# Order of ScalarE's copies, routing counts and a second expert's steps in an attention kernel with two expert layers

## The chip, the cores and the metric

The kernel runs on one core of one Trainium2 chip (trn2). The metric is the device time of one execution in microseconds, of which three were taken: median 483.18 us, lowest 483.08, highest 484.01.

## The reference

Three layers in sequence, all in fp32. (1) Attention over q, k, v of shape 2 x 8 x 768 x 64 with a local window of 96 keys, 8 global keys and a linear bias per head:

```python
scores = scale * np.matmul(q, k.transpose(0, 1, 3, 2))
scores = np.where(keep, scores + bias[None, :, :, :], -1000000000.0)
a = np.exp(scores - np.max(scores, axis=-1, keepdims=True))
out = np.matmul(a / (np.sum(a, axis=-1, keepdims=True) + 1e-09), v)
```

(2) A routed layer: each of the 1536 rows (512 wide) goes to one of 8 experts. A gate decides per row whether it takes its own best expert or that of the row before it. The result is `p[e] * (np.maximum(x @ w1[e], 0) @ w2[e])`, with 512 x 1024 and 1024 x 512 weights per expert. (3) A mixing layer: rows are mixed with the row before them, then `r * (k * k @ w_v)` with `k = np.maximum(xk @ w_k, 0)` and `r` a sigmoid of `xr @ w_r`.

## The kernel before, in words

The program is written under a manual schedule: each engine runs its instructions in the order in which the code emits them, and waits in that order. `n` holds the tensors and routing helpers (class `Net`); the body of `build` emits everything.

**Attention.** 12 tiles t of 128 query rows, each in two halves g of 4 heads: 24 steps i = 2t + g, of which 23 run in the loop `for i in range(NI - 1)` and the last behind it. In a step there are these pieces:

- `emit_S(u)` (L900): scores of step u, 8 products from `strip` (the turned keys, in the trace under zbig) and `qz` (turned, scaled queries). Even u write two S banks, odd u the banks T and O.
- `emit_min(u)` (L914, VectorE): adds the bias table, takes the row minimum of the negated scores, writes the tiles pe (peb, peexh, peexl, or parts of zbig).
- `emit_exp(u, b)` (L926, ScalarE): exponentials with row sums.
- `emit_pT(u, b)` (L933, L935, TensorE): turns the probabilities into a PT bank; `emit_ev(u, b)` copies that bank to pt, for b = 0 on VectorE (L944), for b = 1 on ScalarE (L942).
- `emit_pv(u, b)` (L958): products of pt with v; vp is the part of the tile before. `emit_xT(t)` (L963, ScalarE) copies the finished O bank; `n.turn_x` (L185) turns it and `n.route_x` (L189, VectorE) scales it to the rows X.
- `turn4` (L857) turns the next tile's k and q into two S banks, and `emit_kT` (L862) and `emit_qT` (L866) copy them on ScalarE to `strip` and `qz`.

An odd step from 3 on is "late": it emits the scores of both steps of the next tile, then exponentials, the probabilities of the step before, and so on. An even step turns k and q of the next tile first, then the probabilities of the step before; ScalarE does half of the step's exponentials, the copy pt, the other half, and then the two copies of k and q. The products with v of both halves of a tile end the even step, and the next step's scores follow.

**Routing inside attention.** Tiles go in pairs (groups). Each group runs through gate logits (`route_lgt`, L211), maxima (`route_max`, `route_max2`, tile ab), rows (`route_rows`, L263, ScalarE copy br at L266), a scan over the rows (`route_scan`, L274), turning back (`route_turn`, L282), one-hots (`route_oh`), sums (`route_sum`), positions (`pos`, which computes posi and lets the rows be scattered to xs in DRAM) and a running count (`route_acc`). `plan` is a table: `at(i, point, ...)` registers a function at a named point of step i, `do(i, point)` runs it there. The points of a step in order are Ra, E0 (even steps), Dm, Rb, Db, Rc, Dc; minima of the next step stand between Rb and Db in even steps, the products with v between Db and Rc.

After the groups of tiles 4, 5 and of tiles 6, 7 two experts are picked early: `counted` copies counts, `order_a` makes keys (dgf, dgg), `order_k` compares them on TensorE (L347), `order_c` ranks them (`order_b` is both), `early_pick` (L367) and `early_start` give the expert's number to SP's queue, which then loads its weights (wraw). `scatter` of tile 7 is followed by the load xe of gathered rows on SP (L982), which waits for the scattered rows.

**After attention.** The first expert's tile is computed between the last routing steps (`fill`), then all experts, then the mixing layer. `bg_early` loads and splits the first expert's weights in the late steps of attention.

Of the kernel before, what the change touches and what calls it, by code (L numbers as in the profile page):

```python
# [21 lines left out]
NTT = B * NT  # L22
# [27 lines left out]
NI = 2 * NTT  # L50
# [560 lines left out]
def build(ctx, tc, ins, out):  # L611
    n = Net(ctx, tc, ins, out)
# [247 lines left out]
    def emit_kT(t, psv=None):  # L860
        psv = turn4(kn.pop(t)) if psv is None else psv
        nc.scalar.activation(out=strip[:, :, cols(t):cols(t) + P], in_=psv, func=ACTF.Copy)  # L862
# [110 lines left out]
    def early_start(rank, r):  # L973
        fi = n.early_index(rp, rank)
        wsrc[r] = nc.values_load(fi[:, 0:1], engines=(SP,), min_val=0, max_val=E - 1)
# [23 lines left out]
    def at(i, point, *fs):  # L999
        plan.setdefault((i, point), []).extend(fs)  # L1000

    def do(i, point):
        for f in plan.pop((i, point), ()):
            f()

    def pos(g):
        n.route_pos(ap2, g)
        scq.extend(g)
        nm = {3: "cnt4", 5: "cnt6", 7: "cnte", 9: "cnt9", 11: "cnt"}.get(g[-1])
        if nm:  # L1010
            setattr(n, nm, n.counted(rp, g, nm))

    for g in groups:
        i = 2 * g[-1] + 3
        lgg, mx, mx2, rows, scan, tn, oh, sm_, ps_, acc = (lambda f=f, g=g: f(ap2, g) for f in (
            lambda _, g: n.route_lgt(ap2, g, xTs), n.route_max, n.route_max2, n.route_rows, n.route_scan, n.route_turn, n.route_oh, n.route_sum,
            lambda _, g: pos(g), n.route_acc))
        if g[-1] == NTT - 1:
            tail = mx, mx2, rows, scan, tn, oh, sm_, ps_
            continue  # L1020
        at(i, "Rb", lgg)
        at(i + 1, "E0", lambda g=g: n.route_lge(ap2, g))
        at(i + 1, "Rb", lambda g=g: n.route_lgb(ap2, g))
        at(i + 1, "Db", mx, mx2)
        if g[-1] == NTT - 3:
            tail8 = rows, scan, tn, oh, sm_, ps_, acc
            continue
        if g[-1] == NTT - 5:
            at(i + 1, "Rc", rows)
            at(i + 1, "Dc", scan)  # L1030
            at(i + 2, "Ra", tn)
            at(i + 2, "Dm", oh)
            at(i + 2, "Rb", sm_)
            at(i + 2, "Db", ps_, acc)
        else:
            at(i + 2, "Ra", rows)
            at(i + 2, "Dm", scan)
            at(i + 2, "Rb", tn)
            at(i + 2, "Db", oh)
            at(i + 3, "Rb", sm_)  # L1040
            at(i + 3, "Db", ps_, acc)
        if g[-1] in (5, 7):
            e = g[-1] == 7
            at(i + 3 - e, "Db", lambda e=e: n.order_a(ap2, "fg"[e], n.cnte if e else n.cnt6, n.fvec if e else None))
            if e:
                at(i + 3, "Rb", n.order_k)
                at(i + 3, "Db", lambda: n.order_c(ap2, "g", rp))
            else:
                at(i + 3, "Dc", lambda: n.order_b(ap2, "f", rp))
            at(i + 4, "Ra", lambda e=e: n.early_pick(rp, 3 * e))  # L1050
            at(i + 4, "Dm", lambda e=e: early_start(3 * e, e))

    with tc.manual_schedule():
        n.scalars_load(n.const, nc.scalar)
# [98 lines left out]
        for i in range(NI - 1):  # L1153
# [4 lines left out]
            def scores():  # L1158
# [5 lines left out]
                if i == 0:  # L1164
                    emit_kglob(0)

            turned = []
            if late:
                scores()
                emit_xT(t - 1)  # L1170
                emit_exp(i, 0)
                emit_exp(i, 1)
                do(i, "Ra")
                emit_pT(i - 1, 0)
                emit_pT(i - 1, 1)
                n.turn_x(xTs[t - 1], t - 1, "O" if i < NI - 3 else "PT")
                if i < NI - 2:
                    emit_min(i + 1)
                do(i, "Dm")
                emit_ev(i - 1, 0)  # L1180
                emit_ev(i - 1, 1, True)
            else:
                if i and t + 1 < NTT and not g:
                    turned = [turn4(kn.pop(t + 1)), turn4(qn.pop(t + 1))]
                if 0 < i:
                    emit_pT(i - 1, 0)
                    emit_pT(i - 1, 1)
                do(i, "Ra")
                emit_exp(i, 0)
                do(i, "E0")  # L1190
                if 0 < i:
                    emit_ev(i - 1, 0)
                    emit_ev(i - 1, 1, True)
                emit_exp(i, 1)
                if i and g == 0:
                    n.route_ri(t - 1, stat[t - 1][1])
                do(i, "Dm")
# [4 lines left out]
                scores()  # L1202
            if scq:
                scatter(scq.pop(0))
            if g == 0 and t + 1 < NTT:
                emit_kT(t + 1, *turned[0:1])
                if t + 2 < NTT:
                    load("k", t + 2)
                emit_qT(t + 1, *turned[1:2])
                if t + 2 < NTT:  # L1210
                    load("q", t + 2)
            do(i, "Rb")
            bg_early()
            if i < NI - 2 and not late:
                emit_min(i + 1)
# [58 lines left out]
        i = NI - 1  # L1274
# [755 lines left out]
```

## Time and profile before

| what | value |
|---|---|
| median of 3 runs | 483.18 us (483.08 to 484.01) |
| the profiled execution | 482.91 us |
| its span, first to last instruction | 481.0 us |
| TensorE (PE) busy | 457.8 us, 95% |
| weight loads (PEld) busy | 396.4 us, 82% |
| VectorE (DVE) busy | 345.3 us, 72% |
| ScalarE (ACT) busy | 266.8 us, 55% |
| GpSimd (POOL) busy | 116.4 us, 24% |
| granted TensorE clock | 0.999 of full speed |

Attention and its routing take the first 108 us or so of the span, the experts and the mixing layer the rest. Shares over the whole span say little about one part, so the stretches and timelines below are read by part. In a timeline row, the bracket is the time that the engine sat idle before that instruction and what ended it; "issue" there means that the profile shows no releaser.

### The profile page before, as it was taken

The page shows a single profiled execution, that of the slowest core. Times are in us where ns is not written, and L with a number is a line of the kernel's source. Part 1 is how long each engine was busy: PE and PEld are TensorE (multiplying, and loading weights), DVE is VectorE, ACT ScalarE, POOL GpSimd, SP SyncE. Part 2 cuts the span into 40 slices and gives each one's busy share as a digit, 9 for nine tenths or more (in the row PEclk, how much of TensorE's full clock was granted, in tenths as well). Part 3 has the DMA queues.
Part 4 walks back from the last instruction along what each step waited for, and adds up shares of the span by engine and source line. Part 5 has one row for each costly group of instructions (what it writes and reads, how often), then busy time and mean ns, then how long its engine had stood idle before and what let it go on. Part 6 is the DMA issues. An engine that isn't in the chain of part 4 may idle for free. (4 is left out here: it accounts for less than half of the span.)

```text
span 481.0 us, 9252 instructions
## 1 busy us (share of the span) xinstructions
PE 457.8 (95%) x3210; PEld 396.4 (82%) x3210; DVE 345.3 (72%) x911; ACT 266.8 (55%) x657; POOL 116.4 (24%) x204
## 2 busy tenths in 40 slices
PE   7889989899999999999999999999999999999994
PEld 5778778777788989878879887897989898898984
DVE  7777887896967876988898888797757767363301
ACT  4787877893526645667686775852424324152320
POOL 4202112202210000000010013061854819162220
PEclk9999999999999999999999999999999999999999
DMA  8977485785585878598699743003837441200001
GB/s 191 273 210 170 123 212 177 230 271 167 214 281 162 324 247 310 185 341 286 240 343 399 242 166 110 22 1 98 297 110 256 145 172 62 87 2 23 22 3 49
DMA packets 76491, 86.90 MB, mean 181 GB/s; under 512 B 50676, under 2 KB 50932, under 8 KB 76436
## 3 DMA queue, kind: packets, MB, share of 16 engines
q1 hardware_dynamic: 68176, 63.01, 41.6%
q0 software_dynamic: 4944, 17.17, 10.7%
q10 hardware_dynamic: 3316, 6.03, 3.5%
q8 instruction: 28, 0.46, 0.4%
q14 instruction: 27, 0.22, 0.1%
HBM read 73.49 MB, written 12.71 MB: 179 GB/s over the span
## 5 line engine op out<-in xcount | busy, mean ns | idle before, releaser
L659 ACT ACTIVATE whi<-wraw 128x512 fp32r<-128x512 f32 x128 | 72.5, 623 | 6.5 <-ACT yo L778 2.4
L668 DVE TENSOR_TENSOR wlo<-wraw,whi 128x1024 fp32r<-128x1024 f32 x55 | 66.1, 1218 | 2.7 <-ACT whi L659 2.2
L1541 ACT ACTIVATE sq<-S 128x256 f32<-128x256 f32 x48 | 18.4, 384 | 72.8 <-PE S L677 72.6
L675 PE MATMUL S<-xkh,whi 128*128 128x256 f32 x192 | 54.3, 283 | 0.2 <-ACT whi L659 0.2
L677 PE MATMUL S<-xkh,wlo 128*128 128x256 f32 x192 | 53.3, 278 | 0.2 <-DVE wlo L664 0.2
L1551 POOL TENSOR_TENSOR kl<-sq,kh 128x256 fp32r<-128x256 f32 x40 | 36.4, 919 | 69.5 <-issue 36.7
L676 PE MATMUL S<-xkl,whi 128*128 128x256 f32 x192 | 53.2, 277 | 0.0
L1581 DVE TENSOR_TENSOR o<-O,sig 128x512 f32<-128x512 f32 (+1 forms) x13 | 8.4, 650 | 51.0 <-PE O L677 31.7
L676 PE MATMUL O<-wlo,kh 128*128 128x512 f32 (+1 forms) x104 | 39.1, 376 | 0.6 <-DVE wlo L664 0.6
L677 PE MATMUL O<-whi,kl 128*128 128x512 f32 (+1 forms) x104 | 39.2, 377 | 0.0
L675 PE MATMUL O<-whi,kh 128*128 128x512 f32 (+1 forms) x104 | 38.8, 373 | 0.0
L675 PEld LDWEIGHTS S<-xkh,whi 128*128 128x128 f32 x192 | 36.1, 188 | 0.7 <-ACT whi L659 0.4
L677 PEld LDWEIGHTS S<-xkh,wlo 128*128 128x128 f32 x192 | 36.1, 188 | 0.4 <-DVE wlo L664 0.4
L676 PEld LDWEIGHTS S<-xkl,whi 128*128 128x128 f32 x192 | 36.1, 188 | 0.3
L1542 DVE SCALAR_TENSOR_TENSOR sq<-S,sq 128x256 f32<-128x256 f32 x48 | 20.1, 421 | 15.7 <-ACT sq L1541 15.2
L1550 ACT ACTIVATE kh<-sq 128x256 fp32r<-128x256 f32 x48 | 19.7, 412 | 12.8 <-DVE sq L1542 12.8
L676 PEld LDWEIGHTS O<-wlo,kh 128*128 128x128 f32 x104 | 19.6, 188 | 4.9 <-DVE wlo L664 1.1
L675 PEld LDWEIGHTS O<-whi,kh 128*128 128x128 f32 x104 | 19.6, 188 | 3.6
L307 POOL DMA_INDIRECT xs<-X,posi x10 | 11.4, 1141 | 45.9 <-DVE acc L325 22.0
L942 ACT ACTIVATE pt<-PT 128x512 f32<-128x512 f32 (+1 forms) x24 | 13.5, 561 | 16.3 <-PE PT L935 13.7
L677 PEld LDWEIGHTS O<-whi,kl 128*128 128x128 f32 x104 | 19.6, 188 | 3.5
L944 DVE COPY pt<-PT 128x512 f32<-128x512 f32 (+1 forms) x24 | 15.3, 639 | 5.9 <-PE PT L935 4.7
(485 smaller groups left out, 1420.8 us busy)
## 6 DMA issues: line engine op xcount, KB each, us to landing
wraw<-in_moe_w_dram SPq DMA_DIRECT2D x64, 512.0 KB, 5.3
dwt<-in_moe_w_v_dram POOLq DMA_DIRECT2D x8, 512.0 KB, 4.0
z<-in_moe_w_k_dram SPq DMA_DIRECT2D x8, 512.0 KB, 4.4
z<-in_moe_w_v_dram SPq DMA_DIRECT2D x8, 512.0 KB, 4.9
ys<-yo ACTq DMA_DIRECT2D x13, 256.0 KB, 7.0
vn<-in_v_dram SPq DMA_DIRECT2D x12, 256.0 KB, 3.8
xn<-xs SPq DMA_DIRECT2D x12, 256.0 KB, 5.5
dwt<-in_moe_w_k_dram POOLq DMA_DIRECT2D x6, 512.0 KB, 7.4
```

The costliest lines, as they stand in the source:

```text
L307: self.nc.gpsimd.indirect_dma_start(self.xviews[t], bass.IndirectOffsetOnAxis(ap=self.posi[:, t:t + 1], axis=0), X[t], None)
L659: nc.scalar.activation(out=whl[r, c][0][:, sl], in_=raws[r, c][:, sl], func=ACTF.Copy)
L668: nc.vector.tensor_tensor(lo, raws.pop((r, c)), hi.bitcast(F32), op=ALU.subtract)
L675: nc.tensor.matmul(out_, lhsT=ah, rhs=bh, start=first, stop=False)
L676: nc.tensor.matmul(out_, lhsT=ah, rhs=bl, start=False, stop=False)
L677: nc.tensor.matmul(out_, lhsT=al, rhs=bh, start=False, stop=last)
L942: nc.scalar.activation(out=d[:, 0:ps.shape[1]], in_=ps, func=ACTF.Copy)
L944: nc.vector.tensor_copy(d[:, 0:ps.shape[1]], ps)
L1541: nc.scalar.activation(out=sq_, in_=ps[:, 0:TB], func=ACTF.Relu)
L1542: nc.vector.scalar_tensor_tensor(sq_, ps[:, 0:TB], 0.0, sq_, op0=ALU.max, op1=ALU.mult)
L1550: nc.scalar.activation(out=hh, in_=sq_, func=ACTF.Copy)
L1551: (nc.gpsimd if b else nc.vector).tensor_tensor(hl, sq_, hh.bitcast(F32), op=ALU.subtract)
```

## The change

Four edits, all of order:

1. In even steps from 4 on, the copies of the next tile's k and q (with the loads that follow them) move up, in front of the probabilities' copies pt. The step 2, which had k and q turned first, now turns them behind the probabilities, and copies them where it did before.
2. The counts and keys of both early experts (`counted`, `order_a`) are made at Rb of step 16 and of step 20, in front of the minima; `order_k` follows the products with v (Rc), `order_c` at Dc. Before, the first expert's were at Db and Dc of step 16, the second's spread over Db of step 19 and Rb and Db of step 20.
3. The group of tiles 6, 7 loses its own, earlier slots: its rows move from Rc of step 18 to Ra of step 19 (behind the scores), and all later steps of it half a step or a step on, the scatters of tiles 6 and 7 and the load xe from step 19 to step 20.
4. In step 21 the turn of x moves from in front of the minima's place to behind Rb (behind the gate logits).

```diff
     def pos(g):
...
-        nm = {3: "cnt4", 5: "cnt6", 7: "cnte", 9: "cnt9", 11: "cnt"}.get(g[-1])
+        nm = {3: "cnt4", 9: "cnt9", 11: "cnt"}.get(g[-1])
...
-        if g[-1] == NTT - 5:
-            at(i + 1, "Rc", rows)
-            at(i + 1, "Dc", scan)
-            at(i + 2, "Ra", tn)
-            at(i + 2, "Dm", oh)
-            at(i + 2, "Rb", sm_)
-            at(i + 2, "Db", ps_, acc)
-        else:
...
+        at(i + 2, "Ra", rows)
+        at(i + 2, "Dm", scan)
+        at(i + 2, "Rb", tn)
+        at(i + 2, "Db", oh)
+        at(i + 3, "Rb", sm_)
         if g[-1] in (5, 7):
             e = g[-1] == 7
-            at(i + 3 - e, "Db", lambda e=e: n.order_a(ap2, "fg"[e], n.cnte if e else n.cnt6, n.fvec if e else None))
-            if e:
-                at(i + 3, "Rb", n.order_k)
-                at(i + 3, "Db", lambda: n.order_c(ap2, "g", rp))
-            else:
-                at(i + 3, "Dc", lambda: n.order_b(ap2, "f", rp))
+
+            def count(g=g, e=e):
+                nm = "cnte" if e else "cnt6"
+                setattr(n, nm, n.counted(rp, g, nm))
+                n.order_a(ap2, "fg"[e], getattr(n, nm), n.fvec if e else None)
+
+            at(i + 3, "Rb", count)
+            at(i + 3, "Db", ps_, acc)
+            at(i + 3, "Rc", n.order_k)
+            at(i + 3, "Dc", lambda e=e: n.order_c(ap2, "fg"[e], rp))
...
+            def next_kq(*turned):
+                emit_kT(t + 1, *turned[0:1])
+                if t + 2 < NTT:
+                    load("k", t + 2)
+                emit_qT(t + 1, *turned[1:2])
+                if t + 2 < NTT:
+                    load("q", t + 2)
...
-                n.turn_x(xTs[t - 1], t - 1, "O" if i < NI - 3 else "PT")
+                if i < NI - 3:
+                    n.turn_x(xTs[t - 1], t - 1, "O")
...
-                if i and t + 1 < NTT and not g:
+                if i > 2 and t + 1 < NTT and not g:
                     turned = [turn4(kn.pop(t + 1)), turn4(qn.pop(t + 1))]
...
                 emit_exp(i, 0)
                 do(i, "E0")
+                if turned:
+                    next_kq(*turned)
                 if 0 < i:
                     emit_ev(i - 1, 0)
                     emit_ev(i - 1, 1, True)
...
-            if g == 0 and t + 1 < NTT:
-                emit_kT(t + 1, *turned[0:1])
-                if t + 2 < NTT:
-                    load("k", t + 2)
-                emit_qT(t + 1, *turned[1:2])
-                if t + 2 < NTT:
-                    load("q", t + 2)
+            if g == 0 and t + 1 < NTT and not turned:
+                next_kq()
             do(i, "Rb")
+            if late and i == NI - 3:
+                n.turn_x(xTs[t - 1], t - 1)
```

What the change moves, at three places. ScalarE in step 6, before (lgt are the gate logits, zbig and qz the copies of k and q, peexh and peexl the two halves of the exponentials):

```order
L926 ACTIVATE peexh,sm_561<-peexh,nm_560 128x232 x2
L218 ACTIVATE lgt_605<-R_570 128x256
L942 ACTIVATE pt_1_609<-PT_598 128x512
L926 ACTIVATE peexl,sm_561<-peexl,nm_560 128x232 x2
L862 ACTIVATE zbig<-S_583 128x4x128
L866 ACTIVATE qz<-S_588 128x512
L963 ACTIVATE xT_676<-O_644 128x512
```

and with the change:

```order
L926 ACTIVATE peexh,sm_561<-peexh,nm_560 128x232 x2
L218 ACTIVATE lgt_605<-R_570 128x256
L862 ACTIVATE zbig<-S_583 128x4x128
L866 ACTIVATE qz<-S_588 128x512
L942 ACTIVATE pt_1_615<-PT_598 128x512
L926 ACTIVATE peexl,sm_561<-peexl,nm_560 128x232 x2
L963 ACTIVATE xT_676<-O_644 128x512
```

The two copies now stand in front of pt, and xT follows the exponentials.

TensorE between steps 18 and 19, before (pt with vp ends the products with v, L263 turns the second pair's rows, S, T and O are the scores):

```order
L958 MATMUL O_1486<-pt_1_1447,vn_1126 64x128 x2
L958 MATMUL O_1486<-pt_1_1447,vp 64x128 x2
L263 MATMUL R_1503<-ident,ab_1474 1x128 x4
L900 MATMUL S_1513<-zbig,qz 128x232
L900 MATMUL S_1514<-zbig,qz 128x232
```

and with the change:

```order
L958 MATMUL O_1486<-pt_1_1453,vn_1126 64x128 x2
L958 MATMUL O_1486<-pt_1_1453,vp 64x128 x2
L900 MATMUL S_1504<-zbig,qz 128x232
L900 MATMUL S_1505<-zbig,qz 128x232
L900 MATMUL S_1504<-zbig,qz 128x232
L900 MATMUL S_1505<-zbig,qz 128x232
L900 MATMUL T_1510<-zbig,qz 128x232
L900 MATMUL O_1511<-zbig,qz 128x232
L900 MATMUL T_1510<-zbig,qz 128x232
L900 MATMUL O_1511<-zbig,qz 128x232
L263 MATMUL R_1524<-ident,ab_1474 1x128 x4
```

The rows now come behind all eight products of the scores.

SP's queue around step 20, before (wraw are the first expert's weights, xe the gathered rows, ISA a register step of the load behind it):

```order
L628 DMA wraw_3_1562<-in_moe_w_dram 128x1024
L982 ISA
L982 DMA xe_1593<-xs 128x512
L840 DMA vn_1595<-in_v_dram 128x8x64
L630 ISA
L630 DMA wraw_4_1636<-in_moe_w_dram 128x2x512
L848 DMA vp<-in_v_dram 96x8x64
```

and with the change:

```order
L628 DMA wraw_3_1558<-in_moe_w_dram 128x1024
L840 DMA vn_1570<-in_v_dram 128x8x64
L630 ISA
L630 DMA wraw_4_1623<-in_moe_w_dram 128x2x512
L982 ISA
L982 DMA xe_1664<-xs 128x512
L848 DMA vp<-in_v_dram 96x8x64
```

The load xe now stands behind vn and wraw_4, right ahead of vp.

## Rows read from the trace of the kernel before

**Rows 1.** Windows: length, busy us of PE, PEld, DVE, ACT, POOL, clock, DMA share, GB/s

```profile
24.00:36.00 12.00, 10.62 (x128) 9.05 (x124) 8.53 (x48) 10.19 (x36) 0.58 (x3) 1.00 0.79 210
...
84.00:96.00 12.00, 9.65 (x105) 8.23 (x103) 10.13 (x49) 9.88 (x30) 2.86 (x4) 1.00 0.77 236
96.00:108.00 12.00, 11.35 (x129) 9.05 (x125) 11.32 (x40) 11.23 (x37) 0.57 (x1) 1.00 0.89 268
132.00:144.00 12.00, 12.00 (x60) 9.91 (x59) 7.56 (x13) 3.33 (x6) 1.85 (x3) 1.00 0.87 280
```

**Rows 2.** TensorE's timeline: start, length, instruction, [idle before it <- releaser], rows with a wait

```profile
13.95 0.66 PE L857 MATMUL S<-ident,kn 128*128 128x128 f32 x4 [0.82 <-DVE nm L914]
...
17.91 1.05 PE L900 MATMUL S<-zbig,qz 64*128 64x232 f32 x8 [1.40 <-issue]
...
25.65 1.05 PE L900 MATMUL S<-zbig,qz 64*128 64x232 f32 x8 [0.80 <-issue]
...
34.12 1.05 PE L900 MATMUL S<-zbig,qz 64*128 64x232 f32 x8 [0.58 <-issue]
...
42.71 1.06 PE L900 MATMUL S<-zbig,qz 64*128 64x232 f32 x8 [0.51 <-issue]
...
59.53 1.05 PE L900 MATMUL S<-zbig,qz 64*128 64x232 f32 x8 [0.17 <-issue]
...
66.95 1.05 PE L900 MATMUL S<-zbig,qz 64*128 64x232 f32 x8 [1.29 <-issue]
...
76.03 0.19 PE L347 MATMUL R<-dgf,ones 8*8 8x8 f32 x2 [0.84 <-DVE dgf L339]
...
85.20 0.88 PE L263 MATMUL R<-ident,ab 128*1 128x128 f32 x4 [1.05 <-DVE ab L242]
...
95.19 1.06 PE L900 MATMUL S<-zbig,qz 64*128 64x232 f32 x8 [1.19 <-issue]
```

**Rows 3.** TensorE's timeline: turned q, last product with v, and one at attention's end

```profile
29.95 0.60 PE L857 MATMUL S<-ident,qn 128*128 128x128 f32 x4
...
33.15 0.39 PE L958 MATMUL O<-pt,vp 128*64 128x128 f32 x4
...
106.02 0.39 PE L958 MATMUL O<-pt,vp 128*64 128x128 f32 x4
```

**Rows 4.** ScalarE's timeline in step 2 and in step 6

```profile
15.52 0.38 ACT L942 ACTIVATE pt<-PT 128x256 f32<-128x256 f32 x1 [1.17 <-PE PT L933]
...
31.52 0.60 ACT L942 ACTIVATE pt<-PT 128x512 f32<-128x512 f32 x1 [1.10 <-PE PT L935]
...
33.43 0.59 ACT L866 ACTIVATE qz<-S 128x512 f32<-128x512 f32 x1
33.91 0.60 ACT L963 ACTIVATE xT<-O 128x512 f32<-128x512 f32 x1
```

**Rows 5.** VectorE's timeline: waits, the minima of 68.41, posi of tiles 6 and 7

```profile
47.88 0.69 DVE L189 TENSOR_TENSOR X<-O,RI 128x512 f32<-128x512 f32 x1 [2.02 <-DMA xs<-X,posi]
...
64.25 0.42 DVE L944 COPY pt<-PT 128x256 f32<-128x256 f32 x1 [0.79 <-PE PT L933]
...
68.41 0.39 DVE L914 CUSTOM_DVE_ANT_0 zbig<-S,tb 128x232 f32<-128x232 f32 x1
...
76.26 0.21 DVE L353 TENSOR_SCALAR gtf<-R,keyf 8x8 f32<-8x8 f32 x1 [0.37 <-PE R L347]
...
77.23 0.40 DVE L914 CUSTOM_DVE_ANT_0 peexh<-S,tb 128x232 f32<-128x232 f32 x1 [0.32 <-PE S L900]
...
86.52 0.74 DVE L274 TENSOR_TENSOR_SCAN er<-R,er,br 1x256 fp32r<-1x256 f32 x1 [0.88 <-ACT br L266]
...
90.87 0.17 DVE L319 TENSOR_SCALAR posi<-POS 128x2 int32<-128x2 f32 x1
```

**Rows 6.** SP's queue: issue of the load xe

```profile
96.25 0.34 SPq L982 DMA_DIRECT2D xe<-xs  x1
```

**Rows 7.** Tile vp: from issue to landing of its loads

```profile
DMA to landing us min/median/max: 2.8/3.8/8.0
```

More of the change, by code (lines that the diff above doesn't have):

```diff
@@ L1027, in build @@
             continue
-        if g[-1] == NTT - 5:
-            at(i + 1, "Rc", rows)
-            at(i + 1, "Dc", scan)
-            at(i + 2, "Ra", tn)
-            at(i + 2, "Dm", oh)
-            at(i + 2, "Rb", sm_)
-            at(i + 2, "Db", ps_, acc)
-        else:
[L1036 to L1041, printed above, removed]
+        at(i + 2, "Ra", rows)
[3 more added lines that the diff above has]
+        at(i + 3, "Rb", sm_)
         if g[-1] in (5, 7):
             e = g[-1] == 7
-            at(i + 3 - e, "Db", lambda e=e: n.order_a(ap2, "fg"[e], n.cnte if e else n.cnt6, n.fvec if e else None))
-            if e:
-                at(i + 3, "Rb", n.order_k)
-                at(i + 3, "Db", lambda: n.order_c(ap2, "g", rp))
-            else:
-                at(i + 3, "Dc", lambda: n.order_b(ap2, "f", rp))
+            def count(g=g, e=e):
[6 more added lines that the diff above has]
+            at(i + 3, "Dc", lambda e=e: n.order_c(ap2, "fg"[e], rp))
             at(i + 4, "Ra", lambda e=e: n.early_pick(rp, 3 * e))
             at(i + 4, "Dm", lambda e=e: early_start(3 * e, e))
+        else:
+            at(i + 3, "Db", ps_, acc)
     with tc.manual_schedule():
```

## The prediction

> **What bounds the kernel now.** I read the windows first, to see where an engine has room. From 132 us on TensorE is busy 12.00 of every 12 us and waits for nothing, while in three stretches of the attention part (up to about 108 us) it is busy 9.65 to 11.35 of 12 and VectorE 8.53 to 11.32 [rows 1]. So behind attention the kernel is paced by TensorE, and time that attention saves should arrive at the end nearly whole. The clock was granted in full (1.00) in all these stretches, so it is no term here.
>
> Then I read TensorE's timeline for its waits [rows 2]. Nearly all stand at one place: in front of the scores (S at L900) of an odd step. The releaser is given as "issue", so I looked at what ended last. In the pair of steps around 30 us, TensorE's last product with v ends at 33.15 + 0.39 = 33.54 [rows 3], ScalarE's copy of q starts at 33.43 and the next instruction follows at 33.91 [rows 4], and the scores start at 34.12 [rows 2]. The scores read qz, so it is the copy of q that they wait for. ScalarE meanwhile has idled 1.10 us in that pair, in front of pt at 31.52, waiting for transposed probabilities [rows 4]. The transposes of k and q, which the two copies read, come before those of the probabilities on TensorE: q's begin at 29.95 and take 0.60 [rows 3]. So both copies could have filled that idle time. One copy costs 0.48 there (33.43 to 33.91), two 0.96, against 1.10 of idling.
>
> Two more waits come from routing: at 76.03 TensorE waits 0.84 for dgf (keys of the first expert's order), at 85.20 it waits 1.05 for ab (rows of the second expert's pair) [rows 2].
>
> **The change part by part.** No matrix product, no exponential and no byte of DMA is added or removed; each term is a wait. I take each pair from its own start and ask which engine holds it next.
>
> *Step 2 and the scores at 17.91.* Here the turned k and q now stand behind the probabilities' transposes, so these no longer stand behind a wait of 0.82 for the minima [rows 2]. ScalarE idles 1.17 in front of this pt [rows 4], and all that follows on it up to q's copy is a chain without gaps. It moves ahead by 1.17, less than the 1.40 that the scores wait [rows 2]: 1.2 us.
>
> *Scores at 25.65 and 34.12.* Copies ahead of pt: waits of 0.80 and 0.58 [rows 2]. pt itself is delayed only where the two copies (0.96) exceed the idling; the product with v that reads it is the fourth of four in TensorE's order. So nothing is late in its place. I take 0.7 and 0.5, the rest being the handover from v's products to the scores.
>
> *Scores at 42.71 (wait 0.51).* Nothing. VectorE waits 2.02 us for X at 47.88, released by the landing of scattered rows [rows 5], and the products with v of that pair write the bank that X reads. What comes before gets earlier, the landing does not: 0, at best 0.5. The next pair (scores at about 51) is VectorE's too, which works on from X without a pause through that pair's minima: 0.
>
> *Scores at 59.53 (wait 0.17):* 0.15. *Scores at 66.95 (wait 1.29):* VectorE started at 64.25 after a pause and runs straight through to the minima at 68.41 and on [rows 5]. They start when VectorE is free, not when the scores are there: I take 0.15 of 1.29, the bounds being 0 and 1.29.
>
> *First expert's count in front of the minima.* dgf is then ready long before v's products end, and the 0.84 at 76.03 goes. Three small operations now stand in front of four minima, and posi with the scatters behind it is about half a microsecond later, which nobody waits for there. The gain on VectorE is its two waits at that place, 0.37 and 0.32 [rows 5]: 0.7, bounds 0 and 0.84.
>
> *Second expert's pair behind the scores.* Waits of 1.05 (L263) and 1.19 (scores at 95.19) go from TensorE [rows 2], 2.24 together. But VectorE has only 24.00 - 10.13 - 11.32 = 2.55 us of idling between 84 and 108 [rows 1], of which 0.88 stands at the scan [rows 5]. That scan now follows the minima and finds its row ready, nearly without a wait. Of the other 1.67 I give back little, since order_c, pos and acc pile up behind the minima of step 20, and early_pick at TensorE now waits for them. I take 1.0, bounds 0 and 2.24. The turn of x at step 21, moved behind lgt, avoids a short wait for a bank: nothing on VectorE's path.
>
> *Queues.* The loads of k and q are issued half a step earlier, ahead of a weight load on SP: no cost. The scatters of tiles 6 and 7 come a step later, so on SP xe falls behind vn and a weight load, which are freed, and vp stays behind it. Cost 0 if vp is in time (rival C).
>
> Sum: 1.2 + 0.7 + 0.5 + 0 + 0.15 + 0.15 + 0.7 + 1.0 = 4.4. The profiled execution took 482.91 (span 481.0 and 1.9 around it), which gives 478.5; the median of the three runs is 0.27 above the profiled one, so I say **478.8**.
>
> **Rivals.**
>
> *A. VectorE takes more of it.* From about 60 us on VectorE is so full that the terms after it (0.15 + 0.15 + 0.7 + 1.0 = 2.0) vanish, and 2.4 remain: 480.8. For it: 11.32 of 12 busy between 96 and 108. Against it: VectorE's own waits at 76.26, 77.23 and 86.52 are ended by TensorE and ScalarE [rows 5], and these come earlier. [...] Chance 0.15.
>
> *B. VectorE gives way.* All waits of rows 2 but the 0.82 of step 2, which is within the first term, go: 0.84 + 1.05 + 1.40 + 0.80 + 0.58 + 0.51 + 0.17 + 1.29 + 1.19 = 7.8, so 475.4. Against it: 47.88 and the unbroken run from 64.25. Chance 0.12.
>
> *C. Slower: vp behind xe on SP.* SP is served in order, and xe waits there until the scattered rows have landed: posi ends at 91.04 [rows 5], xe goes out at 96.25 [rows 6], 5.2 us later. In the new order vp goes out right behind xe, about 0.4 later, and the product at 106.02 reads it [rows 3]. Today 106.02 - 91.04 = 15.0 us lie between; posi comes a step later, half of the 8.5 us from scores to scores (25.65 to 34.12), so 10.8 are left. A landing of 3.8 (median) needs 9.4 and is in time; the longest, 8.0 [rows 7], needs 13.6 and stalls TensorE 2.8 us. It decides from a stall over 4.4, a landing beyond 9.6; at 11 the stall is 5.8 and the time 484.6. No row shows such a landing. Chance 0.05; a stall of 1 to 3 us lies in the range.
>
> *D. Given back.* Attention ends earlier, but the first experts' weights or rows don't come sooner, and TensorE waits for them: 483.2. Against it: after 132 us it never waits now, and every load is released by work that moves too. Chance 0.10.
>
> **How the numbers follow.** The forecast, with a gain between 3.2 and 6, has 0.58; A 0.15, B 0.12, C 0.05, D 0.10. The likeliest is 478.8. The range reaches from 476.2 (three quarters of the way to B) to 481.6 (A's time plus a stall of 0.8 as in C), leaving out D, C and part of B. 0.2% is 1.0 us, about what a measurement of this kernel can tell from no change. Faster by more than that: 0.58 + 0.15 + 0.12 = 0.85; within: D, 0.10; slower: C, 0.05.
>
> **What would show it.** In the new profile the two copies (L862, L866) stand right ahead of pt at L942, and ScalarE's 1.1 us in front of pt are nearly gone; TensorE's scores follow v's last product without a wait at about 16.7, 23.8 and 31.7; the pair with X's wait for a landing keeps its length; L347 and L263 wait for nothing at their two places. The product that stands at 106.02 now comes 4 to 5 us earlier, and from there on every stretch has its old length. Wrong would be: waits that reappear in front of v's products (pt late) or in front of T and O's scores (minima late), vp or xe waited for by TensorE near the end of attention, or a gain at 108 us that is not there at the end.

## The result and the profile after

The changed kernel took 479.77 us (median of 4 runs, 478.45 to 480.74), the kernel before 483.6 on the same chip (median of 4); the ratio is 0.9918, 95% interval 0.9890 to 0.9947, so 4.0 us faster by the ratio (3.8 between the medians). A second measurement (6 runs) gave 479.83 us and 0.9908 (0.9875 to 0.9942), 4.5 us. Forecast were 478.8, a gain of 4.4, and a range of 476.2 to 481.6.

The busy times are almost the old ones (TensorE 457.8 before); what went are waits:

```profile
PE 459.8 (96%) x3210; PEld 397.4 (83%) x3210; DVE 344.9 (72%) x911; ACT 266.8 (56%) x657; POOL 115.5 (24%) x204
```

TensorE's timeline of the changed kernel, rows that answer to [rows 2, 3] (start, length, instruction, [idle before it <- releaser]):

```profile
14.42 0.66 PE L857 MATMUL S<-ident,kn 128*128 128x128 f32 x4 [0.25 <-DVE nm L914]
...
17.13 1.05 PE L900 MATMUL S<-zbig,qz 64*128 64x232 f32 x8 [0.28 <-ACT qz L866]
...
24.05 1.05 PE L900 MATMUL S<-zbig,qz 64*128 64x232 f32 x8
...
31.86 1.05 PE L900 MATMUL S<-zbig,qz 64*128 64x232 f32 x8
...
67.77 0.38 PE L282 MATMUL R<-ones_r,er 1*128 1x8 f32 x2 [0.79 <-DVE er L274]
...
72.62 0.19 PE L347 MATMUL R<-dgf,ones 8*8 8x8 f32 x2 [0.21 <-DVE mm L315]
...
82.44 0.60 PE L263 MATMUL R<-ident,ab 128*1 128x128 f32 x4
...
90.58 0.19 PE L347 MATMUL R<-dgg,ones 8*8 8x8 f32 x2 [1.59 <-DVE mm L315]
90.70 1.05 PE L900 MATMUL S<-zbig,qz 64*128 64x232 f32 x8
...
94.84 0.66 PE L185 MATMUL PT<-ident,xT 128*128 128x128 f32 x4 [0.60 <-DVE pt L944]
...
96.64 0.33 PE L933 MATMUL PT<-ident,zbig 128*128 128x128 f32 x1 [0.71 <-DVE X L189]
...
101.98 0.39 PE L958 MATMUL O<-pt,vp 128*64 128x128 f32 x4
...
104.11 0.47 PE L675 MATMUL S<-whi,exexh 128*128 128x512 f32 x1
```

The waits of 1.40, 0.80 and 0.58 in front of the scores are 0.28, none and none; the 0.84 at L347 is 0.21, and the 1.05 at L263 and the 1.19 in front of the last scores (now at 90.70) are gone. The product with vp that stood at 106.02 starts at 101.98. But a wait of 1.59 has come, at 90.58, in front of the second expert's keys, and the one of 0.79 at 67.77 waits for VectorE.

ScalarE in step 6 of the changed kernel, which answers to [rows 4]: both copies, and then pt with no wait listed.

```profile
28.70 0.59 ACT L862 ACTIVATE zbig<-S 128x512 f32<-128x512 f32 x1
29.18 0.60 ACT L866 ACTIVATE qz<-S 128x512 f32<-128x512 f32 x1
...
29.91 0.60 ACT L942 ACTIVATE pt<-PT 128x512 f32<-128x512 f32 x1
```

Windows of the changed kernel, columns as in [rows 1]:

```profile
24.00:36.00 12.00, 12.00 (x134) 10.36 (x131) 9.46 (x50) 10.56 (x36) 1.59 (x6) 1.00 1.00 252
84.00:96.00 12.00, 9.74 (x115) 8.18 (x112) 10.27 (x43) 10.15 (x29) 2.54 (x3) 1.00 0.85 256
96.00:108.00 12.00, 10.73 (x115) 8.80 (x117) 11.66 (x43) 8.92 (x27) 0.76 (x1) 1.00 0.65 203
```

At 24 to 36 TensorE is now full (12.00, before 10.62). At 84 to 108 it still idles 2.26 and 1.27 us, while VectorE is busy 11.66 in the second: there the waits were exchanged rather than removed (2.35 and 0.65 of idling before).

**Where the time came from.** An execution's first scores come 6.5 to 7.5 us into the span, by what the start of the program took, so the places below are counted from the first scores of the same execution (6.88 before, 7.33 after). Each column is one start on TensorE, named by its time in [rows 2] or in the trace of before; L675 is the first expert's first product.

| run | 17.91 | 25.65 | 42.71 | 66.95 | 76.15 | 86.00 | 95.19 | L675 |
|---|---|---|---|---|---|---|---|---|
| before | 11.03 | 18.77 | 35.83 | 60.07 | 69.27 | 79.12 | 88.31 | 101.27 |
| the change | 9.80 | 16.72 | 32.56 | 55.72 | 65.41 | 73.34 | 83.37 | 96.78 |
| the change, again | 9.88 | 17.58 | 33.42 | 56.39 | 66.25 | 74.18 | 84.22 | 97.18 |
| e1_copies | 9.88 | 16.92 | 32.76 | 55.91 | 66.39 | 76.24 | 84.18 | 98.00 |
| e2_routing | 11.03 | 18.77 | 35.83 | 60.24 | 68.86 | 77.45 | 87.82 | 100.78 |
| e3_kpbank | 9.80 | 17.13 | 32.96 | 56.25 | 65.83 | 73.76 | 82.13 | 97.36 |
| e4_step2first | 9.56 | 17.19 | 33.02 | 56.52 | 66.19 | 74.12 | 84.14 | 97.62 |
| e5_first_only | 9.88 | 17.63 | 33.46 | 56.80 | 66.48 | 76.33 | 84.26 | 97.74 |
| e6_fill_sp | 9.83 | 16.70 | 32.54 | 56.10 | 65.71 | 73.64 | 83.67 | 97.15 |
| e11_early | 9.59 | 16.72 | 32.57 | 55.75 | 65.41 | 73.34 | 83.37 | 96.89 |

At L675 the change has gained 101.27 - 96.78 = 4.49 us. From there on all kernels do the same work, in 371.9 to 374.4 us from the first expert's first product chain (L677) to the end; the profile of before is near the low end (481.0 - 108.69 = 372.3), the first profile of the change at the high one (479.0 - 104.65 = 374.4), and its first scores come 0.45 later, so only 2.0 of its 4.49 show in its span. The second one gains 4.09 at L675 and shows 3.8 in its span of 477.2. The two profiles of the same changed program differ by 1.4 behind L677 (374.4 and 372.95), so no loss of the change's is shown there.

### The profile page after: what moved, and what is told of

It reads as the page before. It is cut to its first block, busy times and chain, and to the rows that moved or that the text cites. A ratio compares the mean times of both kernels' runs of the same rounds, so it can differ in the third digit from the quotient of the medians.

```text
span 479.0 us, 9256 instructions
## 1 busy us (share of the span) xinstructions
PE 459.8 (96%) x3210; PEld 397.4 (83%) x3210; DVE 344.9 (72%) x911; ACT 266.8 (56%) x657; POOL 115.5 (24%) x204
## 3 DMA queue, kind: packets, MB, share of 16 engines
q0 software_dynamic: 4944, 17.17, 11.0%
## 4 chain that ended last, share of the span: by engine, by line
PE 34%; issue 9%; DVE 5%; DMA 2%; ACT 2%; POOL 1%; POOLq 0%; ACTq 0%; DVEq 0%
PE S L675 5%; PE S L677 5%; PE S L676 5%; PE O L676 4%; PE O L677 4%; PE O L675 4%; PE PT L677 2%; PE PT L676 2%; PE PT L675 2%; DMA dwt<-in_moe_w_v_dram 1%; DVE wlo L668 1%; DMA yg<-ys,yposi 1%; ACT whi L659 1%; PE T L1490 1%; DVE wlo L664 1%
## 5 line engine op out<-in xcount | busy, mean ns | idle before, releaser
L675 PE MATMUL S<-xkh,whi 128*128 128x256 f32 x192 | 54.6, 284 | 0.2 <-ACT whi L659 0.2
L677 PE MATMUL S<-xkh,wlo 128*128 128x256 f32 x192 | 53.4, 278 | 0.2 <-DVE wlo L664 0.2
L677 PE MATMUL O<-whi,kl 128*128 128x512 f32 (+1 forms) x104 | 39.2, 377 | 0.0
L675 PE MATMUL O<-whi,kh 128*128 128x512 f32 (+1 forms) x104 | 39.0, 375 | 0.0
L675 PEld LDWEIGHTS S<-xkh,whi 128*128 128x128 f32 x192 | 36.2, 188 | 0.8 <-ACT whi L659 0.4
L677 PEld LDWEIGHTS S<-xkh,wlo 128*128 128x128 f32 x192 | 36.1, 188 | 0.4 <-DVE wlo L664 0.4
L675 PEld LDWEIGHTS O<-whi,kh 128*128 128x128 f32 x104 | 19.6, 188 | 3.7
L677 PEld LDWEIGHTS O<-whi,kl 128*128 128x128 f32 x104 | 19.6, 188 | 3.6
L958 PE MATMUL O<-pt,vn 128*64 128x128 f32 x192 | 18.8, 281 | 0.5 <-DVE X L189 0.3
```

Source lines behind the costliest of these rows:

```text
L675: nc.tensor.matmul(out_, lhsT=ah, rhs=bh, start=first, stop=False)
L677: nc.tensor.matmul(out_, lhsT=al, rhs=bh, start=False, stop=last)
L958: nc.tensor.matmul(Os[t][a * HD:(a + 1) * HD, p * P:(p + 1) * P], lhsT=src[:, h * HD:(h + 1) * HD], rhs=d[:, (2 * c + a) * P:(2 * c + a + ...
```

## The experiments

Each kernel was compared with runs of before on the same chip; a gain in us is what the ratio makes of the median of these. Places of L675 and of scores are those of one profile per kernel.

**The whole change again, and its two halves.**

> The changed kernel once more, as the yardstick for the others on the same chip. Expected: 3.8 us faster than before, give or take 1 (the ratio shown with the change was 0.9918, 0.989 to 0.9947).

Measured: 479.83 us, 4.5 faster than before (0.9875 to 0.9942). As expected.

> Before, with edit 1 alone (copies of k and q ahead of pt; step 2 turns k and q behind the probabilities). Theory: the terms of step 2, 25.65, 34.12, 59.53 and 66.95 come (1.2 + 0.7 + 0.5 + 0.15 + 0.15 = 2.7 us), with the 0.5 at 42.71 that the new trace shows kept, 3.2; so 2.5 to 3.3 us faster than before. TensorE's waits of 1.05 at L263 and 0.84 at L347 stay. Rival (the routing edits bring nothing, VectorE swallows them): as fast as the whole change, 3.8. Second rival (the two parts need each other, since VectorE paces 61 to 75 us): under 2.

Edit, in before: `next_kq`, its call behind E0 and `i > 2`, as in the change's diff, and nothing else. Measured: 480.01 us, ratio 0.9923 (0.9893 to 0.9952), 3.7 faster; at L675 101.27 - 98.00 = 3.3. By the time alone the first rival (3.8) fits as well as the theory; the trace and e2 below speak for the theory. The routing's waits stay, and one for vp is new; that load went out at 94.32, and its landing took 8.2 us:

```profile
72.84 0.19 PE L347 MATMUL R<-dgf,ones 8*8 8x8 f32 x2 [0.84 <-DVE dgf L339]
...
82.00 0.88 PE L263 MATMUL R<-ident,ab 128*1 128x128 f32 x4 [1.05 <-DVE ab L242]
...
102.61 0.44 PE L958 MATMUL O<-pt,vp 128*64 128x128 f32 x4 [0.34 <-DMA vp<-in_v_dram]
```

> The changed kernel without edit 1 (edits 2, 3 and 4 alone). Theory: the first expert's 0.7 and the second expert's pair's 0.6 (the trace after shows 0.63 where 1.0 was forecast) come, 1.0 to 1.7 us faster than before, and the waits of 1.40, 0.80 and 0.58 in front of the scores stay. Rival (VectorE swallows the routing terms): within 0.4 of before. Second rival (parts need each other): over 2 faster, or slower than before.

Edit: the change with those lines taken back. Measured: 483.26 us, ratio 0.9975 (0.9953 to 0.9997), 1.2 faster; 0.49 at L675. So edit 1 is some three quarters of the gain or more, and both halves nearly add up (3.3 + 0.5 against 4.1 and 4.5 at L675; 3.7 + 1.2 against 4.0 and 4.5 in the time), though by their times edit 1 alone and the whole change are not told apart. That the routing part buys no less on top of edit 1 (98.00 - 96.78 = 1.2, or 0.8 with the re-run) than alone (0.5 at L675) speaks against rival A, by which it should have bought nothing there.

**The new wait at L347.**

> The changed kernel, with the comparison of keys (order_k, L347) of both early experts written to a PT bank in place of the single R bank that VectorE's mm is still reading. Theory: the new wait of 1.59 us in front of it at 90.58 is this bank's and goes, the scores behind it start earlier; VectorE has a pause of 0.61 at 94 and takes the rest back, so 0.5 to 1.2 us faster than the changed kernel, and another 0.2 at most from the first expert's place. Rival (VectorE, behind with posi and acc, sets the pace at that place): the wait at L347 goes but TensorE then waits as long for the next minima, within 0.2 of the changed kernel.

```diff
-    def order_k(self):
-        self.kp = self.bank("R", 1)
+    def order_k(self, tag="R", bufs=1):
+        self.kp = self.bank(tag, bufs)
...
-            at(i + 3, "Rc", n.order_k)
+            at(i + 3, "Rc", lambda: n.order_k("PT", 2))
```

Measured: 479.68 us, ratio 0.9896 (0.9860 to 0.9932), not told apart from the change; L675 at 97.36, where the change has 96.78 and 97.18. TensorE's timeline of e3:

```profile
89.45 0.20 PE L347 MATMUL PT<-dgg,ones 8*8 8x8 f32 x2
89.58 1.05 PE L900 MATMUL S<-zbig,qz 64*128 64x232 f32 x8
...
92.46 0.18 PE L367 MATMUL R<-Rg,iota_p 8*1 8x1 f32 x2 [0.47 <-DVE Rg L356]
...
101.39 0.66 PE L685 MATMUL S<-ident,xe 128*128 128x128 f32 x4 [0.86 <-DMA xe<-xs]
```

The wait of 1.59 is gone, so it was the R bank's, which mm still reads behind the minima, and the last scores come earlier: 82.13 - 73.76 = 8.37 us behind those of 86.00, where the change takes 10.03. But then 0.47 stand at L367 for VectorE's Rg and 0.86 at L685 for the load xe, and L675 comes 15.23 behind the last scores instead of 13.41 and 12.96. The rival holds in its outcome, not in its place: TensorE does not wait for the next minima, it waits later. VectorE has no pause over 0.2 us from 86.77 on to 106 in e3, and none from 86.27 to 104.5 in the second profile of the change (the first has one, of 0.61 at 94.09).

**The second expert's pair alone.**

> The changed kernel with the second expert's pair (tiles 6, 7) put back to its old places; edit 1 and the first expert's counts in front of the minima stay. Theory: the first expert's part is worth 0.7, the pair's move 0.6: the first expert's first product (L675) starts about 97.4 us behind the first scores (97.2 with the whole change, 98.0 with edit 1 alone), the waits of 1.05 at L263 and about 1.2 in front of the scores near 91 are back, and 1.59 at L347 is gone; 0.2 to 0.8 us slower than the changed kernel. Rival (VectorE, which runs without a pause from 86 to 104 us, sets the end of attention whatever the order in it): within 0.2. Second rival (the pair's move is the whole of the routing gain): L675 at 98.0.

Edit: in the change the old slots of the group of tiles 6, 7 and the old places of its order (those that the change's diff removes). Measured: 479.68 us, ratio 0.9933 (0.9910 to 0.9955), not told apart from the change. L675 at 97.74 against 97.18 in the re-run, both with equally late third scores (17.63, 17.58). That is 0.56, but 0.23 of it stand already at the scores of 76.15 (66.48 and 66.25), up to which both kernels do the same, so 0.33 are left. From those scores to L675 the old places take 31.61 (e1) and 31.26 (e5), the new ones 30.93 to 31.48 in five profiles (the change, its re-run, e4, e6, e11). A gain of the pair's move is thus not told apart from none.

**What is left in the early steps.** In the re-run the third scores stand at 17.58, 0.86 behind the first profile's 16.72. ScalarE and TensorE of the re-run:

```profile
19.32 0.60 ACT L942 ACTIVATE pt<-PT 128x512 f32<-128x512 f32 x1 [0.51 <-PE PT L935]
19.32 1.59 ACTq L1239 DMA_DIRECT2D xs<-warm  x2
20.96 0.49 ACT L926 ACTIVATE zbig<-zbig,nm 128x232 f32<-128x232 f32 x1 [1.04 <-DVE X L189]
...
22.88 0.59 ACT L942 ACTIVATE pt<-PT 128x512 f32<-128x512 f32 x1
```

```profile
23.52 0.44 PE L958 MATMUL O<-pt,vn 128*64 128x128 f32 x4 [0.60 <-ACT pt L942]
```

ScalarE of the first profile at the same place:

```profile
20.04 0.82 ACTq L1239 DMA_DIRECT2D xs<-warm  x2
20.91 0.49 ACT L926 ACTIVATE zbig<-zbig,nm 128x232 f32<-128x232 f32 x1 [0.27 <-issue]
...
22.42 0.83 ACTq L1239 DMA_DIRECT2D xs<-warm  x2
22.82 0.59 ACT L942 ACTIVATE pt<-PT 128x512 f32<-128x512 f32 x1
23.30 0.49 ACT L926 ACTIVATE zbig<-zbig,nm 128x232 f32<-128x232 f32 x1
```

ScalarE issues two DMAs (L1239, they fill xs) behind pt; in the re-run the issues took 1.59 us and ScalarE stood idle for 1.04 in front of the exponentials behind them, in the first profile 0.82 and 0.27. The next two issues, at 22.42, cost no idle time. The next pt is late by 0.86, counted from the first scores, and the products with v wait 0.60. The exponentials start when the second issue is out (19.32 + 1.59 = 20.91); the releaser printed, X, had ended half a microsecond before.

> The changed kernel with the eight DMAs that fill xs (L1239, steps 1 to 4) issued on SP in place of ScalarE. In the re-measured run ScalarE stood still for 1.04 us behind its copy pt at 19.32 while two of these issues took 1.59, and the products with v waited 0.60 for the next pt; in the first profile of the change the two took 0.82 and nothing waited. Theory: with the copies of k and q ahead of pt, ScalarE has no slack left there, so the issues are now on the path: the wait in front of v's products near 23.5 goes in every run, the third scores start at 16.6 to 16.8 us behind the first (16.7 to 17.6 in the runs so far), 0 to 0.8 us gained, and more even runs. Rival (SP's loads of k, q and v come later behind them, or the issue time is only the queue's and takes as long elsewhere): the wait stays, or TensorE waits for kn or qn near 20 to 25 us.

```diff
-                    nc.scalar.dma_start(out=n.xs[e * REG:e * REG + PRE, :], in_=n.warm)
+                    nc.sync.dma_start(out=n.xs[e * REG:e * REG + PRE, :], in_=n.warm)
```

Measured: 479.84 us, ratio 0.9933 (0.9912 to 0.9954), no change that could be told in the time. In the trace the theory holds: third scores at 16.70, no wait in front of v's products. But the pair of 42.71 to 51 takes 0.3 longer, by X's wait (X starts 5.61 behind posi, in the first profile 5.28), and L675 stands at 97.15. That is not the edit's: with the same edit e11 has 5.27 there.

> The changed kernel, but step 2 treated as the steps from 4 on: k and q turned first and copied ahead of pt. Theory: what step 2 gained came from getting the probabilities' transposes out from behind the turned k, which waits for the minima (0.82 before); with k and q first again that wait is back and stands in front of pt and the products with v, so the second scores start 0.4 to 0.9 us later than in the changed kernel (10.3 to 10.7 us behind the first scores, where it is 9.8 to 9.9), and the time is 0.4 to 0.9 longer. Rival (it is the copies' place on ScalarE that counts, in step 2 too): the second scores start at the same time or earlier.

```diff
-                if i > 2 and t + 1 < NTT and not g:
+                if i and t + 1 < NTT and not g:
```

Measured: 479.09 us, ratio 0.9900 (0.9873 to 0.9926). My theory fell: the wait of 0.82 is back, and yet the second scores come at 9.56, 0.3 earlier than with the change (9.80, 9.88). It is the copies' place that counts in step 2 too; putting the turned k and q behind the probabilities there cost 0.3 at the second scores. Further on nothing of the 0.3 is seen: the third scores come at 17.19, behind a wait of 0.44 for pt as in the re-run, and L675 at 97.62.

> The changed kernel with the two edits that held in the early steps: step 2 turns k and q first and copies them ahead of pt as all later steps do (e4), and the fills of xs are issued on SP (e6). Theory: both waits are gone at once, the second scores start 9.5 to 9.6 us behind the first (9.8 to 9.9 with the change) and the third 16.4 to 16.5 (16.7 to 17.6 with the change); 0.3 to 1.2 us faster than the changed kernel by the trace, as far as the later wait for X's scatter lets it through. Rival (that wait, and VectorE behind it, swallows all of it): L675 within 0.2 of 97.2 behind the first scores, the time that of the changed kernel.

Edit: e4 and e6 together. Measured: 479.53 us, ratio 0.9915 (0.9894 to 0.9935). Second scores at 9.59 as expected, third at 16.72 and not 16.4; L675 at 96.89. The rival holds in the outcome (0.3 before its 97.2, 0.1 behind the first profile's 96.78): the 0.2 gained at the second scores is gone at the third, though no wait over 0.2 us stands between them, and nothing of it reaches L675.

**VectorE in the last steps.**

> The changed kernel with three of the background subtractions (wlo, L664, 128x512, 0.6 us each) of the last steps of attention on GpSimd in place of VectorE, all between 87 and 98 us. Theory: VectorE, which there runs without a pause from 86 to 104, sets the pace, so taking 1.8 us off it brings the first expert's first product (L675) 0.6 to 1.5 us forward, from 97.2 to 96.6 or less behind the first scores. Rival (TensorE's order or the landing of the gathered rows xe sets the end of attention): L675 within 0.2 of 97.2, and VectorE has pauses where the subtractions were. Second rival (GpSimd slows VectorE while it works): later than 97.2.

```diff
-    def w_lo1(r, c, s):
+    def w_lo1(r, c, s, eng=nc.vector):
...
-        nc.vector.tensor_tensor(lo[:, sl], raws[r, c][:, sl], hi[:, sl].bitcast(F32), op=ALU.subtract)
+        eng.tensor_tensor(lo[:, sl], raws[r, c][:, sl], hi[:, sl].bitcast(F32), op=ALU.subtract)
...
-                w_lo1(0, *lo_q.pop(0))
+                w_lo1(0, *lo_q.pop(0), nc.gpsimd if keep and u[1] else nc.vector)
```

Measured: 478.54 us, ratio 0.9887 (0.9860 to 0.9914), the lowest median here, but its interval overlaps the change's. From the scores of 86.00 to those of 95.19 it takes 85.11 - 75.65 = 9.46 us where the change takes 10.03: 0.57 less, about the length of the one subtraction (0.65) that stood ahead of them, and the wait at L347 falls from 1.59 to 1.03. So VectorE's work does set the pace there, by way of the R bank: with the bank free, e3 takes 8.37 with the subtraction still on VectorE. Behind these scores more than the gain is lost again: L675 comes 14.53 behind them (13.41 and 12.96 with the change), so by the trace the theory fell, and the low median stays without an explanation. The second rival is seen once, with 0.32 us (last section). One wait there is for a load:

```profile
92.44 0.19 PE L347 MATMUL R<-dgg,ones 8*8 8x8 f32 x2 [1.03 <-DVE mm L315]
...
105.13 0.44 PE L958 MATMUL O<-pt,vp 128*64 128x128 f32 x4 [1.03 <-DMA vp<-in_v_dram]
```

> e7_lo_pool with the load of vp issued in front of xe on SP. In e7's profile xe left SP only at 98.94 and vp behind it at 99.39, and the product with vp waited 1.03 at 105.13; with edit 1 alone it waited 0.34. Theory: this is rival C's mechanism, a wait for SP's order and not for the memory, so vp leaves SP near 91 us, lands before it is needed, and no product waits for vp; L675 0.3 to 1.0 us earlier than in e7 (14.5 us behind the scores of step 21 there), and the time 0 to 1.0 shorter than e7's. Rival (the wait for vp covered another, for the next transposed probabilities or for xe): another wait of about 1 us stands there instead, and the time is e7's.

Edit, on e7: the two lines with `load_vp(t + 1)` ahead of the loop over `scq[:2]`. Measured: 480.33 us, ratio 0.9909 (0.9880 to 0.9937). SP and TensorE of e8:

```profile
91.63 0.62 SPq L848 DMA_DIRECT2D vp<-in_v_dram  x1
...
99.58 0.35 SPq L982 DMA_DIRECT2D xe<-xs  x1
```

```profile
105.23 0.66 PE L685 MATMUL S<-ident,xe 128*128 128x128 f32 x4 [2.21 <-DMA xe<-xs]
```

vp leaves 7.8 us earlier than in e7 and nothing waits for it: it was SP's order. In its place TensorE waits 2.21 for xe, whose load is held until the scattered rows have landed (scatters issued at 93.37 and 94.69). The rival holds, and the loss is larger than it says: L675 comes 17.17 behind the last scores, in e7 14.53. From the issue of xe to the product that reads it 5.65 us pass here, in e7 at most 3.75 (98.94 to 102.69, without a wait); why the load took longer no run shows. The profiled execution was the slowest of e8's twelve (484.19 us).

> e8 with the key comparison in a PT bank (as e3) and the fills of xs on SP (as e6). Theory: with 1.8 us less on VectorE there, the wait of 1.03 at L347 that is left in e7 is no longer covered by VectorE, so removing it now pays 0.4 to 1.0 us where it paid nothing in e3, and the wait in front of v's products in step 4 (0 to 0.8) goes too: 0.4 to 1.8 us faster than e8, L675 at 95.5 or less behind the first scores. Rival (the landing of xe sets the end of attention, as e3's wait of 0.86 there): L685 waits for xe and L675 stays within 0.3 of e8's.

Edit: e8 with those of e3 and e6. Measured: 479.57 us, ratio 0.9910 (0.9882 to 0.9938). The scores of 95.19 come another 1.09 earlier (83.72 - 75.35 = 8.37 against e8's 9.46), and L685 waits 2.16 for xe. L675 comes 2.4 earlier than in e8 (100.05 against 102.46), which is more than the rival allows, but 16.33 behind the last scores, where the change needs 13.41: what was gained on the way (8.37 against 10.03) is lost again before it, in the main at the load. The stretch of 8.37 is the same in e3, with all subtractions on VectorE, so taking them away adds nothing there once the bank is free.

> e9 with the turn of the gathered rows xe (L685) behind the turn of x and four of v's products, some 1.4 us of TensorE's work that does not read xe, instead of ahead of them. Theory: if L685 waits for the landing of xe in e9, that wait is covered by this work, and L675 comes earlier by up to as much as the wait, 0.3 to 1.0 us. Rival (the halves of xe that ScalarE and VectorE make from L685's output, 1.3 us of work, now come later than L675 wants them): L675 waits for exexh, no gain or up to 0.5 slower.

Edit, on e9: `next(first_rows)` goes, and the loop over `first_rows` stands behind `emit_pv(i - 1, 1)`. Measured: 482.12 us, ratio 0.9971 (0.9944 to 0.9997). L685 waits no longer, but ScalarE, in order, idles 1.77 in front of the copy of xe and its exponentials come late: TensorE waits 0.84 for them, and L675 gains 0.36. Its runs are 2.5 us longer than e9's though its profile is not: the profiled execution is a typical one of e10's (481.88) and the slowest of e9's (482.11). Four of e10's twelve runs list a mean granted clock of 0.983 to 0.992, but the other eight have a median of 482.0 too, so the cause stays open. e7 to e10 were profiled in executions that started slowly (last section).

No version is shown to beat the change.

## Why the prediction was right, and where its terms were not

The sum was 4.4 us at the end of attention; the traces give 4.49 and 4.09, the time 4.0 and 4.5. The mechanism of edit 1 was right, and it is most of the gain. That the sum came out so close is in part luck: a gain of 0.56 that was set to nothing makes up for terms at the end that were too large. The terms, as gains at their place:

- **Step 2:** forecast 1.2, measured 11.03 - 9.80 = 1.23. Its reason was half right: e4 gets 11.03 - 9.56 = 1.47 without the part that I argued from.
- **25.65 and 34.12:** forecast 0.7 and 0.5, measured 0.82 and 0.66 (in the re-run 0.04 and 0.66, the first lost to the two DMA issues). The copies filled ScalarE's idle time, as the rows above show.
- **42.71:** forecast 0, measured 0.56. This step of the prediction failed: "What comes before gets earlier, the landing does not". Taken at its word it would have cost the 2.4 us of the terms before it too, which the sum kept. VectorE of before and of the change, then GpSimd of both:

```profile
42.38 0.17 DVE L319 TENSOR_SCALAR posi<-POS 128x2 int32<-128x2 f32 x1
```

```profile
40.13 0.17 DVE L319 TENSOR_SCALAR posi<-POS 128x2 int32<-128x2 f32 x1
...
45.41 0.69 DVE L189 TENSOR_TENSOR X<-O,RI 128x512 f32<-128x512 f32 x1 [2.37 <-DMA xs<-X,posi]
```

```profile
42.84 1.30 POOL L307 DMA_INDIRECT xs<-X,posi  x1 [6.62 <-DVE posi L319]
```

```profile
40.60 1.31 POOL L307 DMA_INDIRECT xs<-X,posi  x1 [6.63 <-DVE posi L319]
```

The scatter is issued 0.46 and 0.47 behind posi, and X starts 5.50 behind posi before, 5.28 after, and 5.26 to 5.85 in all profiles. Posi is VectorE's and had moved by 2.25 in the span, 2.70 counted from the first scores, so the landing moved with it. A wait for a transfer is fixed only if its issue is.

- **59.53 and 66.95:** forecast 0.15 each. Edit 1 alone has gained 2.84 at the scores of 51, 2.81 at those of 59.53 (52.65 and 49.84 behind the first), 4.16 at those of 66.95 and 2.88 at those of 76.15. So the first term brought nothing, and the 1.29 go at their place and are given back in the next step but for 0.07: VectorE takes them, as argued, and rival B fell here. Between the two waits at its pt and at gtf VectorE works for 12.0 us before (64.25 to 76.26 [rows 5]) and as long in e1:

```profile
61.12 0.42 DVE L944 COPY pt<-PT 128x256 f32<-128x256 f32 x1 [0.79 <-PE PT L933]
...
73.06 0.21 DVE L353 TENSOR_SCALAR gtf<-R,keyf 8x8 f32<-8x8 f32 x1 [0.37 <-PE R L347]
```

- **First expert's count:** forecast 0.7. At the scores of 76.15 and 86.00 the change is 0.98 and 2.90 ahead of e1, where it had been 0.19 ahead at 66.95; as the wait of 1.05 at L263 is moved in that stretch too, the first figure is the cleaner one, about 0.8. From 66.95 to 76.15, where only this edit tells them apart, e5 is 0.80 shorter than e1, and e2 0.58 shorter than before.
- **Second expert's pair:** forecast 1.0. Against before it measures 0.63 (4.49 - 3.86), in the re-run 1.07 (4.09 - 3.02); against e5 it is 0.33, and against e1 and e5 together within their spread. So the term is not shown to have come. The sum had no price for the R bank, a single one, in which `order_k` now follows sums that mm reads only behind the minima: 1.59 us of wait, where the prediction had L347 wait for nothing. Nor is the bank alone what was missing: e3 frees it, gains 1.66 at the last scores and nothing at L675, since VectorE's work and the load xe lie under it.
- **Queues:** cost 0, as seen. In the change xe goes out at 95.57 and vp at 96.02, and 101.98 waits for nothing; rival C fell. Its mechanism is real, though: 1.03 in e7, gone in e8. The 0.34 in e1 are another case, a landing of 8.2 us in the old order; before, the same load took 8.0 and was just in time (97.81 to 105.8).
- **Rival A** fell: behind the scores of 59.53, where by it nothing more comes, the change gains another 1.33 and the re-run 1.76 (4.49 - 3.16 and 4.09 - 2.33), of 2.0 forecast. **Rival D** fell by the times and by the re-run, which keeps 3.45 of its 4.09 behind L677 (its later work takes 372.95 against 372.3).

The Trainium skill ("Perfetto Trace Analysis", section "Identifying the Most-Contended Engine") would have the engine with the highest occupancy optimized first, TensorE being judged by its weight loads. At 84 to 108 us, where that is VectorE, the runs agree in part: waits of 2.24 taken from TensorE bought 0.33 to 1.07, not told apart from nothing, and 0.65 taken from VectorE moved the last scores by 0.57, though not L675. At 24 to 36 the fullest engine is ScalarE (10.19 of 12 against VectorE's 8.53 and 9.05 of weight loads [rows 1]), and the gain came from its order, every wait of TensorE's there being for its copies, which agrees.

## What to carry to other kernels

Where an engine idles in front of one instruction while the next ones have their inputs, move these ahead, and check what else sits between: two DMA issues in the same stream held ScalarE up for 0.27 to 1.04 us at one place and not at all at the next. Before a term is set to 0 because something "waits for a transfer", look at what issues the transfer; and before a pair of steps is moved, list the single buffers that it shares with its new neighbours. Near the end of a stage several waits lie under one another (bank, VectorE, xe, vp): taking one away uncovers the next, so the sum of the rows (2.24 here) can be far more than what comes.

## What the hardware showed that I had not expected

**A slow start.** In the profiles of e7 to e10 TensorE's products before about 13 us took longer, and the second scores, counted from the first, come 1.7 to 1.95 us later than with the change. The re-run of the change and e7:

```profile
4.87 0.70 PE L1067 MATMUL O<-warm 128*128 128x256 f32 x2
...
6.53 0.71 PE L900 MATMUL S<-zbig,qz 64*128 64x128 f32 x8 [0.53 <-ACT qz L876]
```

```profile
4.90 1.22 PE L1067 MATMUL O<-warm 128*128 128x256 f32 x2
...
7.45 1.22 PE L900 MATMUL S<-zbig,qz 64*128 64x128 f32 x8 [0.47 <-ACT qz L876]
```

The same instructions take 0.70 and 0.71 in one, 1.22 and 1.22 in the other, and small products 0.38 and 0.63, with a granted clock of 1.00 (2.4 GHz) listed in both from 4 to 14 us. What TensorE did until then (warm products from 1.53 on) is the same. How long it lasts differs between executions of one program: in the first profile of the change the warm product takes 1.22 too, and the scores behind it 0.71. e7's profiled execution took 481.20 us and its four others 477.92 to 478.94. But all four profiles with subtractions on GpSimd start slowly for so long and none of the other ten, so that the kernel has no part in it is not shown. The Trainium skill ("TensorE: Matmul & The Clock Gate", section "What's actually happening") has the number of slow products at the start of one kernel vary from run to run, which agrees with the two profiles of the change.

**GpSimd and VectorE.** The subtraction of 128x512 took 1.27 us on GpSimd, 0.65 on VectorE. Beside it one small VectorE operation of e7 took 0.48 instead of the 0.16 that it takes in the re-run, and ended when GpSimd's did (99.15):

```profile
97.88 1.27 POOL L664 TENSOR_TENSOR wlo<-wraw,whi 128x512 fp32r<-128x512 f32 x1 [1.10 <-ACT whi L659]
```

```profile
98.69 0.48 DVE L194 TENSOR_SCALAR RI<-sm 128x8 f32<-128x8 f32 x1
```

That agrees with the Trainium skill ("SBUF — State Buffer", section "Who interferes with whom"), by which the two engines share ports, and an operation of VectorE that needs the shared ones (`tensor_scalar` can be one) blocks until GpSimd has finished, or the other way round. The copies of VectorE that read PSUM took their 0.68 to 0.69 beside GpSimd's subtractions.

**DMA issues on a computing engine.** Two issues took 0.82 to 1.59 us on ScalarE in the profiles of the same program, and held it up for 0.27 to 1.04 us, at the next place not at all. The Trainium skill ("DMA: Bandwidth & Descriptors", section "Issuing engines are not separate DMA queues") calls the time of an issue usually small against the transfer. Single issues of 0.34 to 1.21 us against 3.8 to the landing (the re-run) agree with that in the main; but what counts for an engine that computes is its own time, and 1.04 us is more than the 0.48 that a copy costs it.
